# Moving an RMS gain from the weights to the transposed activations, and re-ordering the first batch, in a fused attention and SwiGLU kernel

## The chip, the cores and the metric

The kernel runs on one core of a Trainium2 chip. A core has five engines that run their own instruction streams in order and meet at semaphores: PE (TensorE, matmuls and transposes), DVE (VectorE), ACT (ScalarE), POOL (GpSimd) and SP (SyncE, which here only issues transfers). Transfers run on 16 DMA engines that all queues share. The metric is device time in microseconds (us) of one execution; lower is better.

## The reference

Selective attention over 8 batches, 8 heads, 576 positions and head size 64, followed by a SwiGLU feed-forward network (FFN) over the resulting 4608 tokens of width 512, with RMS normalisation and a gain `rms_g` in front of it:

```python
scores = scale * np.matmul(q, k.transpose(0, 1, 3, 2))
cum = np.cumsum(np.maximum(s, 0.0), axis=-1)
bias = -(cum[:, :, :, None] - cum[:, :, None, :])
scores = np.where(causal, -1000000000.0, scores + np.minimum(bias, 0.0))
...
attn = attn / (np.sum(attn, axis=-1, keepdims=True) + 1e-09)
x = np.matmul(attn, v)          # then tokens x (heads * 64)
rms = np.sqrt(np.mean(x * x, axis=-1, keepdims=True) + 1e-06)
xn = x / rms * rms_g
g = xn @ w_gate                 # 512 x 1536
silu = g * (1.0 / (1.0 + np.exp(-g)))
out = (silu * (xn @ w_val)) @ w_out
```

## The kernel before

**Units of work.** A batch is cut into five blocks of 128 positions (the last has 64). For each batch `b`:

- k and q arrive as fp32 over SP's queue (`load_kq`, `load_kq_tail`) in one buffer `kq32` for all batches, and are cast to bf16 in ten pieces (`cast`, L133, into `kqn`, which holds two batches). V arrives as bf16 over POOL's queue, one transfer a block (`load_v`, L137).
- Eight steps T (`t_step`, L146) transpose a pair of heads of k (w = 0) or q (w = 1) through PSUM into `kqT`: four PE transposes and one copy, on ACT or DVE (L154, L152). A tail step (L161, L164, L165) does the last 64 positions.
- S steps (`s_step`, L196) compute scores of a key block for four heads; ACT takes exp with the decay as a per-partition bias (L212) into `E`; POOL zeroes the causal corner with an affine select (L218), called the mask below.
- AV steps (`av_step`, L233, L239) multiply by V, with a column of ones for the sum. DVE divides (L246, L248), sums squares (L253), POOL raises mean square plus epsilon to the power -1/2 (L256, L259).
- `x_scale` (L266, DVE) applies that factor; an XT step (`xt_step`, L274) transposes the block through PSUM tile `psT`, and one DVE copy (L279) writes `xnT`, a ring that holds four FFN chunks.

The FFN runs in nine chunks of 512 tokens. A chunk has twelve pieces of 128 columns of the gate (L472, then tanh on ACT, L475) and of the value (L481), which DVE joins into `Ht` (L484, L477), and then four output tiles (L496) that ACT copies out (L501). Silu is written with tanh: g(1 + tanh(g/2))/2. The factor 1/2 and `rms_g` are multiplied into the weights by `scale_w` (L515, L518), one half of the columns at a time.

**Order.** Nothing is scheduled by a tool: the order on each engine is the order of the calls. The first part of the program (L585 to L693) is a list written by hand: transfers, setup of the decay (`decay_setup`, which ends in `biasK`), the first four blocks of batch 0, batch 1's casts and transposes. From there on attention is cut into steps that `step` places in the FFN's matmuls, one call of `step` being a slot; a chunk calls it 36 times. `can_t`, `can_s`, `can_av` and `can_xt` say which step may be placed, by lags counted in slots and not by any time. Before a chunk, `need` calls `step` until the XT step of the chunk's last token has been placed, which makes slots without FFN work. V transfers, casts and checks of the input's range (`check_mag`, `check_max`, results in `acc`) wait in side queues (`v_side`, `pool_side`, `dve_side`), from which a slot takes at most one each.

**PSUM.** `psF` has four buffers (FFN tiles, and pairs for early S steps); `psS`, `psAV` and `psT` have one buffer each. A step that writes into one of these waits on PE until its last reader has ended, and PE runs in order.

**A second path.** `general` computes the same without the range assumptions, and runs only if the checks fail; with these inputs it doesn't run.

Of the kernel before, what the change touches and what calls it, by code (L numbers as in the profile page):

```python
# [26 lines left out]
def kernel(  # L27
# [12 lines left out]
    nc = tc.nc  # L40
# [66 lines left out]

    def psT():
        return pp.tile([128, 8, 128], BF16, name="psT", tag="T", bufs=1)

    def psT32():
        return pp.tile([128, 512], FP32, name="psT32", tag="T", bufs=1)

# [21 lines left out]
    def load_v(b, c):  # L135
        n = rows(c)
        nc.gpsimd.dma_start(  # L137
            out=v_sb[0:n, b % 2, c, :, 0:64],
            in_=v[b, :, c * 128:c * 128 + n, :].rearrange("h p d -> p h d"))
# [130 lines left out]
    def xt_step(b, qb):  # L270
# [8 lines left out]
        nc.vector.tensor_copy(out=xnT[:, :, t0:t0 + m], in_=pX[:, 0:CC, 0:m])  # L279
        if m < n:  # L280
            nc.vector.tensor_copy(out=xnT[:, :, 0:n - m], in_=pX[:, 0:CC, m:n])
# [13 lines left out]
    SLOTS = 36  # L295
    slot = [0]
    done = {}
# [23 lines left out]
    def check(b):  # L321
        later(dve_side, 2, [f for w in (0, 1) for f in (
            lambda w=w: check_mag(b, w), lambda: check_max(0), lambda: check_max(1))]
            + [lambda: done.__setitem__(("check", b), slot[0])])
# [19 lines left out]
    def after_av(b):  # L344
        if b + 2 < B:
            later(v_side, 1, [lambda c=c: load_v(b + 2, c) for c in range(NSC)]
                  + [lambda: done.__setitem__(("V", b + 2), slot[0])])

    def do_t(key, **kw):
        b, hp, w = key  # L350
        if hp == "tail":
            tail_step(b)
            done["T", b] = slot[0]
            after_tail(b)
        else:
            t_step(b, hp, w, **kw)
# [26 lines left out]
    def can_t():  # L383
        if not t_seq or slot[0] - last["T"] < 2:
            return False
        b, hp, w = t_seq[0]
        return ready(2, "cast", b) and (b < 2 or ready(1, "S", b - 2, 4, 0))
# [14 lines left out]
    def can_av():  # L402
# [3 lines left out]
        if b > 1 and not ready(8, "V", b):  # L406
# [17 lines left out]
    def step():  # L424
# [9 lines left out]
        if v_side and slot[0] % 2:  # L434
# [29 lines left out]
    def ffn(c, extra=None):  # L464
        x0 = (c * DM) % RING
# [27 lines left out]
        for tb in range(4):  # L493
# [7 lines left out]
            nc.scalar.activation(out=osb, in_=Op, func=AF.Copy)  # L501
# [8 lines left out]

    def scale_w(i):

        fs = slice(i * (DF // 2), (i + 1) * (DF // 2))
        for cc in range(CC):
            nc.vector.tensor_scalar(out=wg_sb[:, cc, fs], in0=wg_sb[:, cc, fs],  # L515
                                    scalar1=rms_g_sb[:, cc:cc + 1], scalar2=None, op0=ALU.mult)
        for cc in range(CC):
            nc.vector.tensor_scalar(out=wv_sb[:, cc, fs], in0=wv_sb[:, cc, fs],  # L518
                                    scalar1=rms_g_sb[:, cc:cc + 1], scalar2=0.5,
                                    op0=ALU.mult, op1=ALU.mult)  # L520

    def decay_setup():
# [10 lines left out]
        ps = psT32()  # L533
# [49 lines left out]
    with tc.manual_schedule():  # L583

        load_kq(nc.sync, 0, 0, 0, 4)  # L585
        nc.scalar.dma_start(out=s_sb, in_=s.rearrange("b h s -> (b h) s"))
        load_kq(nc.scalar, 0, 1, 0, 4)
        load_kq(nc.sync, 0, 0, 4, 8)
        load_kq(nc.scalar, 0, 1, 4, 8)
        for w in (0, 1):  # L590
            load_kq_tail(nc.sync, 0, w)
        nc.sync.dma_start(out=rms_g_sb, in_=moe_rms_g.rearrange("(cc p) -> p cc", p=128))
        make_identity(nc, ident_f)
        make_identity(nc, ident_bf)
        nc.vector.memset(shf[:, 4, 64:128], 0.0)
        nc.vector.memset(v_sb[:, 0, :, :, 64:65], 1.0)
        nc.vector.memset(mhalf, -0.5)
        nc.vector.memset(stat, 0.0)
        nc.vector.memset(kq32[64:128, :, :, 256:320], 0.0)
        nc.vector.memset(ss_all, 0.0)  # L600
        nc.gpsimd.memset(E[:, 6:8, :, 192:256], 0.0)
        load_v(0, 0)
        decay_setup()
        for g in (0, 1):
            h0, h1 = 4 * g, 4 * g + 4
            for w in (0, 1):
                cast(nc.scalar, 0, w, 0, 1, h0, h1)
                cast(nc.vector, 0, w, 1, 2, h0, h1)
                cast(nc.gpsimd, 0, w, 2, 3, h0, h1)
                cast(nc.gpsimd, 0, w, 3, 4, h0, h1)  # L610
            load_v(0, 1 + g)
        load_w(moe_w_gate, wg_sb, 0)
        load_w(moe_w_val, wv_sb, 0)
        for w in (0, 1):
            cast(nc.gpsimd, 0, w, 4, 5)
        done["cast", 0] = 0
        load_v(0, 3)
        load_w(moe_w_gate, wg_sb, 1)
        load_w(moe_w_val, wv_sb, 1)
        for w in (0, 1):  # L620
            load_kq(nc.sync, 1, w)
            load_kq_tail(nc.sync, 1, w)
        nc.vector.memset(v_sb[:, 1, :, :, 64:65], 1.0)
        nc.vector.memset(v_sb[64:128, :, 4, :, 0:64], 0.0)
# [4 lines left out]
        t_seq[:] = [x for x in t_seq if x[0] > 1 or x[1:] == ("tail", 0)]  # L629
        t_seq.pop(0)  # L630
        scaled[0] = 4

        def t_first(b, g):
            for hp in (2 * g, 2 * g + 1):
                for w in (0, 1):
                    do_t((b, hp, w), pT=psF16() if w else psT())
# [4 lines left out]
        def s_first(kb, g, pair=None):  # L641
            do_s((0, kb, g), pair)()

        t_first(0, 0)
        s_first(0, 0)
        t_first(0, 1)
        s_first(0, 1, pairF())
        s_first(1, 0, pairF())
        do_av((0, 0, 0))
        do_av((0, 0, 1))  # L650
        s_first(1, 1)
        s_first(2, 0, pairF())
        do_av((0, 1, 0))
        x_scale(0, 0)
# [235 lines left out]
```

## Time and profile before

| | |
|---|---|
| median of three runs | 421.56 us (420.84 to 422.25) |
| the profiled execution | 420.97 us, of which 419.4 us are the span of the trace |
| PE busy | 371.8 us (89%) |
| DVE busy | 322.2 us (77%) |
| ACT busy | 217.8 us (52%) |
| POOL busy | 180.1 us (43%) |
| first FFN matmul | 47.17 us |
| first matmul of chunk 1 | 100.57 us |
| last PE work ends | 412.9 us |

The times of engines are sums of their instructions. A busy share over the whole span hides that the stages differ: the first 47 us hold no FFN work, the first chunk takes 53 us, and later chunks about 39. Over the span in 40 slices the page shows (one digit a slice, busy tenths; DMA is the mean share of the 16 transfer engines):

```profile
PE   1563779698999889999999999999999999999993
DVE  4458499899899699988897899979767966764740
...
DMA  9999985348931755629242630190020011001002
```

In lists in order of time, a line has the start, the length, the engine, the program's line, the operation, output<-input, the shapes and the count; in brackets stands how long the engine was idle before, and what ended that.

### The profile page before, as it was taken

How to read it: one execution, taken by the hardware profiler on the slowest of the kernel's cores; microseconds unless marked ns; L12 is line 12 of the kernel's file. 1: busy time of each engine (PE TensorE's matmuls, PEld its weight loads, DVE VectorE, ACT ScalarE, POOL GpSimd, SP SyncE). 2: the span in 40 equal slices, each digit the busy share in tenths (PEclk: the TensorE clock that was granted, in tenths of full speed). 3: DMA queues.
4: the chain of work that ended last, by engine and by line, in shares of the span. 5: the costliest groups of instructions: out<-in, count | busy, mean ns of one | idle time of the engine just before them, and what ended most of it. 6: DMA issues, size and time to landing. Idle time of an engine off the chain costs nothing. (4 is left out here: it accounts for less than half of the span.)

```text
span 419.4 us, 7416 instructions
## 1 busy us (share of the span) xinstructions
PE 371.8 (89%) x2679; PEld 183.2 (44%) x2679; DVE 322.2 (77%) x678; ACT 217.8 (52%) x516; POOL 180.1 (43%) x288
## 2 busy tenths in 40 slices
PE   1563779698999889999999999999999999999993
PEld 1342433344544444445445444444454445444441
DVE  4458499899899699988897899979767966764740
ACT  2661265652577647644765486558645753323321
POOL 6767727576717757535734575343221320000000
PEclk9999999899999999999999999999999999999998
DMA  9999985348931755629242630190020011001002
GB/s 241 215 232 256 178 135 36 22 135 211 150 115 50 233 70 50 208 79 81 76 153 76 64 21 25 65 69 2 27 76 2 2 50 52 1 29 73 1 28 80
DMA packets 72125, 38.46 MB, mean 92 GB/s; under 512 B 47440, under 2 KB 67408, under 8 KB 72080
## 3 DMA queue, kind: packets, MB, share of 16 engines
q0 software_dynamic: 41168, 9.44, 24.4%
q1 hardware_dynamic: 29776, 27.27, 20.9%
q10 hardware_dynamic: 1136, 1.20, 0.8%
q8 instruction: 23, 0.38, 0.4%
q14 instruction: 22, 0.18, 0.1%
HBM read 37.90 MB, written 9.44 MB: 113 GB/s over the span
## 5 line engine op out<-in xcount | busy, mean ns | idle before, releaser
L212 ACT ACTIVATE E<-psS,biasK 128x256 bf16<-128x256 f32 (+2 forms) x300 | 105.6, 434 | 33.3 <-PE psS L196 30.6
L472 PE MATMUL psF<-xnT,wg_sb 128*128 128x512 bf16 x432 | 111.9, 382 | 2.0 <-DVE xnT L279 1.1
L481 PE MATMUL psF<-xnT,wv_sb 128*128 128x512 bf16 x432 | 112.8, 384 | 0.5 <-DVE Ht L477 0.2
L496 PE MATMUL psF<-wout_sb,Ht 128*128 128x512 bf16 x432 | 104.9, 379 | 0.0
L475 ACT ACTIVATE T<-psF 128x512 f32<-128x512 f32 x108 | 64.7, 599 | 74.3 <-PE psF L472 62.8
L218 POOL TENSOR_SCALAR_AFFINE_SELECT E<-E 128x512 bf16<-128x512 bf16 x72 | 49.5, 688 | 99.9 <-ACT E L212 98.9
L484 DVE SCALAR_TENSOR_TENSOR U<-T,psF 128x512 bf16<-128x512 f32 x108 | 73.7, 683 | 18.3 <-ACT T L475 17.9
L477 DVE TENSOR_TENSOR Ht<-U,psF 128x512 bf16<-128x512 bf16 x99 | 67.5, 682 | 5.5 <-PE psT L146 0.5
L481 PEld LDWEIGHTS <-wv_sb 128*128 128x128 bf16 x432 | 39.3, 98 | 45.4 <-issue 6.9
L472 PEld LDWEIGHTS <-wg_sb 128*128 128x128 bf16 x432 | 38.1, 98 | 39.0 <-issue 7.2
L496 PEld LDWEIGHTS <-Ht 128*128 128x128 bf16 x432 | 37.8, 98 | 38.0 <-issue 2.7
L133 POOL CAST kqn<-kq 128x512 bf16<-128x512 f32 (+1 forms) x80 | 51.7, 669 | 4.0 <-DMA kq<-in_k_dram 2.3
L501 ACT ACTIVATE osb<-psF 128x512 f32<-128x512 f32 x36 | 21.6, 601 | 48.6 <-PE psF L496 45.0
L256 POOL TENSOR_SCALAR al_all<-ss_all 128x1 f32<-128x1 f32 (+1 forms) x40 | 15.9, 397 | 62.8 <-DVE xs_sb L253 62.2
L248 DVE TENSOR_TENSOR x_sb<-psAV,rZ 128x256 bf16<-128x256 f32 (+1 forms) x80 | 33.8, 423 | 2.7
L239 PE MATMUL psAV<-v_sb,E 128*128 128x65 bf16 x320 | 30.2, 199 | 5.9 <-POOL E L218 5.9
L137 POOL DMA_DIRECT2D v_sb<-in_v_dram x40 | 35.3, 889 | 0.0
L233 PE MATMUL psAV<-v_sb,E 128*128 128x65 bf16 x256 | 25.7, 198 | 6.9 <-DVE x_sb L248 6.9
L196 PE MATMUL psS<-kqT 64*128 64x256 bf16 (+2 forms) x300 | 25.7, 257 | 6.3 <-ACT E L212 4.9
L253 DVE SCALAR_TENSOR_TENSOR xs_sb<-x_sb 128x512 bf16<-128x512 bf16 (+1 forms) x40 | 29.7, 743 | 1.4
L154 ACT ACTIVATE kqT<-psT 128x512 bf16<-128x512 bf16 x32 | 19.4, 607 | 19.9 <-PE psT L146 19.9
L239 PEld LDWEIGHTS <-E 128*128 128x128 bf16 x320 | 22.8, 101 | 14.3 <-POOL E L218 6.4
(82 smaller groups left out, 318.2 us busy)
## 6 DMA issues: line engine op xcount, KB each, us to landing
out_dram<-osb SPq DMA_DIRECT2D x36, 256.0 KB, 2.0
kq<-in_k_dram SPq DMA_DIRECT2D x7, 1024.0 KB, 5.9
kq<-in_q_dram SPq DMA_DIRECT2D x7, 1024.0 KB, 6.7
v_sb<-in_v_dram POOLq DMA_DIRECT2D x32, 128.0 KB, 4.4
wg_sb<-in_moe_w_gate_dram POOLq DMA_DIRECT2D x2, 768.0 KB, 15.0
wv_sb<-in_moe_w_val_dram POOLq DMA_DIRECT2D x2, 768.0 KB, 19.5
wout_sb<-in_moe_w_out_dram POOLq DMA_DIRECT2D x1, 1536.0 KB, 14.7
kq<-in_k_dram SPq DMA_DIRECT2D x2, 512.0 KB, 5.2
```

Source lines behind the costliest of these rows:

```text
L133: eng.tensor_copy(out=o, in_=i)
L137: nc.gpsimd.dma_start(out=v_sb[0:n, b % 2, c, :, 0:64], in_=v[b, :, c * 128:c * 128 + n, :].rearrange("h p d -> p h d"))
L212: nc.scalar.activation(out=Ev[:, h - h0, 0:N], in_=pair[par][:, o:o + N], func=AF.Exp, scale=0.125, bias=biasK[:, kb, bh:bh + 1])
L218: nc.gpsimd.affine_select(out=Ev[:, :, 0:nq], in_=Ev[:, :, 0:nq], pattern=[[0, nh], [1, nq]], compare_op=ALU.is_ge, fill=0.0, base=0, chan ...
L239: nc.tensor.matmul(o, lhsT=d, rhs=v_sb[:, p, qb, h, :], start=(j == 0 and qb == 0), stop=(j == 3))
L248: nc.vector.tensor_tensor(out=xo[:, g * 256:(g + 1) * 256].rearrange("p (h d) -> p h d", h=4), in0=pv[0:n, :, 0:64], in1=rZ[0:n].unsqueeze ...
L472: nc.tensor.matmul(Gp, lhsT=wg_sb[:, cc, fs], rhs=xnT[:, cc, x0:x0 + DM], start=(cc == 0), stop=(cc == CC - 1))
L475: nc.scalar.activation(out=T, in_=Gp, func=AF.Tanh, scale=0.5)
L477: nc.vector.tensor_tensor(out=Ht[:, fb - 1, :], in0=pend[0], in1=pend[1], op=ALU.mult)
L481: nc.tensor.matmul(Vp, lhsT=wv_sb[:, cc, fs], rhs=xnT[:, cc, x0:x0 + DM], start=(cc == 0), stop=(cc == CC - 1))
L484: nc.vector.scalar_tensor_tensor(out=U, in0=T, scalar=1.0, in1=Gp, op0=ALU.add, op1=ALU.mult)
L496: nc.tensor.matmul(Op, lhsT=Ht[:, fb, tb * 128:(tb + 1) * 128], rhs=wout_sb[:, fb, :], start=(fb == 0), stop=(fb == FB - 1))
```

## The change

`scale_w` is gone. `rms_g` is applied where `xnT` is written: each of the four groups of 128 model columns has the gain as a per-partition scalar there, so a block's copy becomes four, two on ACT and two on DVE. The factor 1/2 rides in the copy of the output tile. The hand-written first part is re-ordered: casts of batch 0 split differently over the engines, transposes of heads 0 to 3 first, V transfers and weight transfers placed between other work on POOL, batch 1's k cast on ACT and q on POOL, batch 1's transposes left to the slots (with a lag of one slot, alternating between `psT` and the bank of `psAV`), some memsets on other engines, all first k and q loads on SP's queue. V's readiness is now kept for each block, the V queue may run in each of the first eight slots, and the checks' marker shares its last entry.

```diff
@@ xt_step
-        nc.vector.tensor_copy(out=xnT[:, :, t0:t0 + m], in_=pX[:, 0:CC, 0:m])
-        if m < n:
-            nc.vector.tensor_copy(out=xnT[:, :, 0:n - m], in_=pX[:, 0:CC, m:n])
+        for d0, j0, j1 in ((t0, 0, m), (0, m, n)):
+            if j1 == j0:
+                continue
+            for cc in range(CC):
+                o, i = xnT[:, cc, d0:d0 + j1 - j0], pX[:, cc, j0:j1]
+                if cc < 2:
+                    nc.scalar.activation(out=o, in_=i, func=AF.Copy, scale=rms_g_sb[:, cc:cc + 1])
+                else:
+                    nc.vector.tensor_scalar(out=o, in0=i, scalar1=rms_g_sb[:, cc:cc + 1],
+                                            scalar2=None, op0=ALU.mult)
@@ load_v
+        done["V", b, c] = slot[0]
@@ do_t
+            if b == 1 and (hp + w) % 2:
+                kw["pT"] = psAV16()
@@ can_t
-        if not t_seq or slot[0] - last["T"] < 2:
+        if not t_seq:
             return False
         b, hp, w = t_seq[0]
+        if slot[0] - last["T"] < (1 if b == 1 else 2):
+            return False
@@ can_av
-        if b > 1 and not ready(8, "V", b):
+        if not ready(8, "V", b, qb):
@@ step
-        if v_side and slot[0] % 2:
+        if v_side and (slot[0] % 2 or slot[0] < 9):
@@ ffn
-            nc.scalar.activation(out=osb, in_=Op, func=AF.Copy)
+            nc.scalar.activation(out=osb, in_=Op, func=AF.Copy, scale=0.5)
@@ the first part, after the change (transfers, memsets and setup cut)
+        for g in (0, 1):
+            for w in (0, 1):
+                load_kq(nc.sync, 0, w, 4 * g, 4 * g + 4)
...
+        piece(0, 0, (ACT, ACT, POOL, POOL))
+        decay_setup()
+        piece(1, 0, (ACT, DVE, POOL, POOL))
         load_v(0, 0)
+        do_t((0, 0, 0), pT=psT(), dve=True)
+        do_t((0, 1, 0), pT=psF16(), dve=False)
+        do_t((0, 0, 1), pT=psAV16(), dve=True)
+        do_t((0, 1, 1), pT=psF16(), dve=False)
+        piece(0, 1, (ACT, DVE, DVE, POOL))
         load_w(moe_w_gate, wg_sb, 0)
+        piece(1, 1, (ACT, DVE, DVE, POOL))
         load_w(moe_w_val, wv_sb, 0)
+        s_first(0, 0)()
...
+        load_v(0, 1)
+        s_first(0, 1, pairF())()
+        s_first(1, 1)()
         for w in (0, 1):
+            cast(POOL, 0, w, 4, 5)
+        do_av((0, 0, 0))
+        do_av((0, 0, 1))
+        load_v(0, 2)
+        s_first(2, 0, pairF())()
+        tail_step(0)
...
+        x_scale(0, 1)
+        load_w(moe_w_gate, wg_sb, 1)
+        do_av((0, 2, 0))
+        do_av((0, 2, 1))
+        load_w(moe_w_val, wv_sb, 1)
+        s_first(3, 1, pairF())()
+        do_xt((0, 1))
...
+        for r in range(NSC):
+            cast(ACT, 1, 0, r, r + 1)
+        x_scale(0, 2)
+        do_av((0, 3, 0))
+        do_av((0, 3, 1))
+        do_xt((0, 2))
+        nc.gpsimd.memset(v_sb[64:128, :, 4, :, 0:64], 0.0)
+        x_scale(0, 3)
+        for r in range(NSC):
+            cast(POOL, 1, 1, r, r + 1)
+        do_xt((0, 3))
...
+        later(v_side, 0, [
+            lambda: load_v(0, 4), lambda: load_v(1, 0), lambda: load_v(1, 1),
+            lambda: nc.gpsimd.dma_start(out=wout_sb,
+                                        in_=moe_w_out.rearrange("(fc p) d -> p fc d", p=128)),
+            lambda: load_v(1, 2), lambda: load_v(1, 3), lambda: load_v(1, 4)])
...
-            if fb == 3:
-                scale_w(1)
```

`piece(w, g, engines)` casts rows 0 to 3 of k (w = 0) or q (w = 1) for heads 4g to 4g + 3, one row on each engine named. The setup's PE transposes go to a `psF` buffer instead of `psT`. `general` gets the same treatment of `rms_g` and 1/2.

## The prediction

> **What bounds the kernel now.** I read the stretches first (busy time of each engine between marks that I set at the first feed-forward matmul, at the long stops of TensorE and at the start of chunk 1), then the order in time around each stop. Columns of the stretches: start:end, length, busy time (instructions) of PE, its weight loads, DVE, ACT, POOL, then granted clock, DMA share and GB/s.
>
> ```profile
> 0.00:47.17 47.17, 20.95 (x182) 14.56 (x183) 27.46 (x66) 19.29 (x46) 34.67 (x60) 1.00 1.15 235
> 47.17:59.67 12.50, 12.49 (x74) 5.19 (x72) 9.06 (x16) 7.55 (x22) 3.83 (x5) 1.00 1.43 155
> 59.67:62.07 2.40, 0.25 (x8) 0.26 (x9) 2.37 (x8) 0.79 (x3) 1.18 (x1) 1.00 0.40 66
> ...
> 75.80:78.67 2.87, 0.00 (x1) 0.00 (x1) 2.06 (x7) 2.84 (x10) 0.00 (x0) 0.91 0.68 43
> 78.67:100.57 21.90, 19.42 (x160) 9.58 (x160) 20.41 (x45) 9.94 (x27) 14.14 (x22) 0.93 0.52 155
> ```
>
> Two stages differ from the rest. Before 47.17 no FFN matmul runs and PE is busy 20.95 of 47.17 us. Chunk 0 (47.17 to 100.57, 53.4 us) is 14 us longer than a later chunk (about 39), with DVE busy 46.4 of it, so DVE is the nearest limit there. After 100.57 PE is busy all but some 6 us up to 413, so what is won or lost before 100.57 reaches the end almost whole.
>
> In the first stage POOL, DVE and PE show what stands in front of the FFN:
>
> ```profile
> 28.02 2.84 POOL L133 CAST kqn<-kq 128x512 bf16<-128x512 f32 x5
> 31.54 3.69 POOL L133 CAST kqn<-kq 128x512 bf16<-128x512 f32 x5 [0.69 <-DMA kq<-in_q_dram]
> 35.19 0.75 POOL L218 TENSOR_SCALAR_AFFINE_SELECT E<-E 128x512 bf16<-128x512 bf16 x1
> ```
> ```profile
> 32.97 2.48 DVE L515 TENSOR_SCALAR wg_sb<-wg_sb,rms_g_sb 128x768 bf16<-128x768 bf16 x4
> 35.37 1.76 DVE L518 TENSOR_SCALAR wv_sb<-wv_sb,rms_g_sb 128x768 bf16<-128x768 bf16 x4
> ```
> ```profile
> 35.99 0.24 PE L239 MATMUL psAV<-v_sb,E 128*128 128x65 bf16 x1 [3.79 <-POOL E L218]
> ...
> 43.96 0.61 PE L274 MATMUL psT<-ident_bf,xs_sb 128*128 128x128 bf16 x4 [1.51 <-DVE xs_sb L266]
> 45.09 0.59 PE L146 MATMUL psT<-ident_bf,kqn 128*128 128x128 bf16 x4 [0.52 <-DVE xnT L279]
> ```
>
> The reader sees batch 1's ten casts ahead of a mask on POOL, so that attention-times-V waits 3.79 us; DVE scaling weights (4.24 us) just after; and batch 1's transposes (L146) ahead of the FFN.
>
> **The change, part by part.**
>
> *Start of the FFN.* The last exps of batch 0's first four blocks end at 33.0 (31.64 + 1.36). With no casts, weight scaling or batch-1 transposes in between, the chain from there is: mask 0.65, AV 0.4, L246 + L248 + L253 at 0.18 + 0.42 + 0.83, power (L256, L259) 0.82, L266 0.6, transposes 0.6, then the new copies to xnT about 1.0 (below): 5.5 us, so 38.5. The first stage also starts sooner. All casts and transposes of heads 0 to 3 are placed first: biasK is ready at 9.67 as now (the s transfer is the same), one cast on DVE 0.42, two pairs of transposes 1.1, copy 0.6, so the first score matmul comes at 11.8 instead of 13.37, 1.6 us sooner. That gives 37.0. ACT's five new casts (128x512; the POOL rows give 0.6 to 0.74, I take 0.6: 3.0 us) lie after the last exps and end about when the third block's transposes are ready: nothing, and up to 2 us if ACT is late. POOL keeps five casts, now behind the last power and a memset of V (L624's row: 0.9): 4.6 us. They begin 2.2 us before the FFN (L266, transposes, copies) and the second slot needs them 3.4 us after its start (rows at 47.17 and 48.87, 1.7 each): 5.6 us of cover; what exceeds it stops PE one for one. Memsets that change engines: acc (POOL 2.23) goes to DVE's 2.98 idle before s lands, about 1.1 by L599's row; kqT's goes to DVE, about 0.5, in front of an L266 that waits for the power: nothing.
>
> *Queues.* The first four k and q loads all go to SP's queue, s alone to ACT's. They landed at 5.7 to 10.9 and move the same bytes, without V piece 0 beside them; the casts they feed wait for biasK at 9.67. I take nothing, bounds -1 and +0.5. wout is now issued on POOL behind the mask of slot 3, near 47, and lands 14.7 later (its row); the output matmuls are 36 us behind the start, at 74: hidden.
>
> *The V transfers.* POOL's queue shows one order. I asked for each transfer by its issue time; the last column is us to landing, issue times 13.39 and 15.24:
>
> ```profile
> wv_sb<-in_moe_w_val_dram POOLq DMA_DIRECT2D x1, 768.0 KB, 13.5
> ...
> v_sb<-in_v_dram POOLq DMA_DIRECT2D x1, 128.0 KB, 16.6
> ```
>
> So a V piece issued behind two weight halves landed at 31.8, 4.9 us after the half before it (26.9); the half before that landed at 22.0, 4.1 after the V piece before. Now V piece 1 moves from ahead of the weights to behind them (issue about 16.5). Weights are issued near 9 and 10, piece 0 lands about 12, the halves about 16 and 21, piece 1 between 22.2 (five V pieces issued from 44.5 land 1.2 apart) and 25.9 (the 4.9). PE wants it at 22.5: late by 0 to 3.4 us, and everything in that row of work with it. I take 1.5, as batch 1's q is stuck behind the k tail until POOL's tail casts and is only starting then. FFN start: 37.0 + 1.5 = 38.5, a gain of 8.7 (bounds 5.5 to 11). The second weight halves, issued near 30 and 31, land by 45 with the same 5 us each; the FFN reads them 15 us after its start: hidden.
>
> *Chunk 0.* Out: the second weight scaling, 2.8 us of DVE (58.5 to 61.2), PE's stop of 2.4. In: eight transpose steps of batch 1, PE 0.22 each when warm (102.30 to 102.52) = 1.8, four copies on DVE of 0.69 = 2.8, four on ACT. DVE is unchanged and DVE limits: I take 0; bounds -2.4 (only PE counts as stopped) and +1.8 (only PE's work counts). The steps alternate between psT and psAV; twice one follows a user of the same buffer by one slot or less, so PE can stand for a DVE copy (0.7 each), inside these bounds.
>
> *xnT.* Forty copies of 128x512 (0.41) or 128x256 (0.28) become two on ACT and two on DVE. The two DVE sizes give 0.15 + 0.0005 per element, 0.2 for 128 columns: two cost 0.4, nothing new. ACT's exps at 64 and 192 columns take 0.22 and 0.34 each in a row, so 0.28 for 128, 0.56 a block, on an engine busy 52%. The wait is what matters. The tail step already has this form, ACT and DVE reading one psT:
>
> ```profile
> 28.00 0.38 ACT L164 ACTIVATE kqT<-psT 128x256 bf16<-128x256 bf16 x1 [0.71 <-PE psT L161]
> ```
> ```profile
> 28.41 0.29 DVE L165 COPY kqT<-psT 128x256 bf16<-128x256 bf16 x1 [1.52 <-ACT kqT L164]
> ```
>
> DVE starts only when ACT has ended, though both only read. So a block's copies take 0.56 + 0.4 = 1.0 in place of 0.41, and DVE, with Ht and U queued behind, stands for up to 0.6 a block; PE waits for U and Ht through psF. Where DVE lags, it finds ACT done and pays nothing. In chunk 0 (four blocks, two of DVE's largest users around) I take 0.3 each, 1.2; in the other chunks DVE has 23.7 us idle from 100.57 to 294, so most is covered: 1.0. Bounds 0 and 5.
> [...]
>
> *Boundary to chunk 1.* The planner's rules, followed slot by slot, put batch 1's attention later: the FFN's chunk 1 begins at slot 40 instead of 37 (a chunk fills 36), chunk 2 at 77 instead of 76. Empty slots leave PE to the chain AV, L246 to L266, transposes, xnT. Now that stop is 0.96 + 0.68 us (99.5 to 100.57). I take +1.0 (bounds 0 and 2.5), and -0.5 where the next boundary loses two empty slots. A stop can also cool PE: after 2.92 us idle, four matmuls took 1.89 instead of 1.03 and the whole stretch 1.3 more, after 2.4 idle they took 1.02. [...]
>
> *Nothing:* the 0.5 at the output rides in an ACT copy that is there anyway (L501, 0.60).
>
> Sum: -8.7 + 0 + 1.2 + 1.0 + 1.0 - 0.5 = -6.0. The profiled execution took 420.97 (span 419.4 and 1.6 around it), so 415.0; the median of the runs is 0.6 above that execution: **415.6**.
>
> **The rivals.**
> 1. *V late* (15%). Piece 1, then pieces 2 and 3, land as late as the 4.9 rows allow, and the FFN starts at 42: gain 2.5, 419. For: two halves ahead in one queue. Against: they are issued 3 us sooner than now.
> 2. *DVE was not the limit of chunk 0* (20%). The removed stop counts (-2.4), copies hide, start at 37: 415.6 - 1.5 - 2.4 - 1.2 = 410.5. For: PE stopped exactly while L515 and L518 ran. Against: DVE 93% busy from 78.67 on.
> 3. *The ACT-to-DVE order on psT makes it slower* (7%). 36 blocks in the FFN stage; if each leaves DVE standing 0.35 that PE feels, 12.6 in place of 2.2, giving 426. It decides from about 0.25 a block, where the 8.2 us won otherwise are eaten. For: DVE is 85 to 93% busy to 294. Against: ACT is idle 38% there and usually first.
> 4. *Moved work only* (3%): stops reappear in chunk 0, about 421.
>
> **How the numbers follow.** My forecast has 55%, by itself 412.5 to 418.5. The range 410 to 420.5 takes in most of rivals 1 and 2 and leaves out rival 3 and a start near 36. A difference under 0.3% (1.3 us) can't be told from none. Faster: 55 + 20 + 11 of rival 1; same: 4 of rival 1 and 3 of rival 4; slower: rival 3.
>
> **What would show it.** The first FFN matmul near 38.5; the AV of block 1 in batch 0 naming a V transfer as releaser for 0 to 3 us; DVE's xnT pieces naming ACT; no stop of 2.4 us in chunk 0; chunk 1 starting 93 to 95. Wrong if the FFN starts after 42, or if chunk 0 exceeds 57 us.

## The result

| | before | after |
|---|---|---|
| median | 421.46 us | 429.0 us (428.18 to 429.2) |
| ratio to before, 95% interval | | 1.0174 [1.0152, 1.0196] |
| profiled execution / its span | 420.97 / 419.4 us | 428.18 / 426.6 us |
| first FFN matmul | 47.17 us | 43.92 us |
| chunk 0 | 53.40 us | 56.83 us |
| chunks 1 to 8 | 312.30 us | 318.11 us |
| end of PE's work to end of the span | 6.5 us | 7.7 us |

The change makes the kernel 1.7% slower, where 1.4% faster was predicted. The rows of the table account for the 7.2 us between the two spans: -3.25 + 3.43 + 5.81 + 1.2. The FFN does start sooner, but chunk 0 takes the same time back, and the later chunks lose nearly 6 us more.

The stretches of the kernel after, cut at the first FFN matmul of a chunk (start:end, length, busy time and instructions of PE, its weight loads, DVE, ACT, POOL, granted clock, DMA share, GB/s):

```profile
0.00:43.92 43.92, 16.95 (x150) 10.85 (x151) 22.77 (x59) 20.98 (x54) 24.25 (x47) 1.00 1.00 194
43.92:100.75 56.83, 45.28 (x352) 21.91 (x352) 47.31 (x104) 32.76 (x88) 30.95 (x47) 1.00 0.89 153
100.75:146.18 45.43, 42.99 (x312) 20.73 (x312) 38.04 (x76) 29.19 (x75) 25.96 (x41) 0.96 0.60 127
146.18:194.12 47.94, 42.49 (x340) 20.88 (x340) 40.72 (x98) 28.39 (x74) 22.64 (x40) 1.00 0.45 93
194.12:418.86 224.74, 223.09 (x1531) 106.56 (x1528) 170.43 (x372) 127.21 (x315) 64.07 (x110) 1.00 0.24 48
```

And chunks 1 and 2 (rows 3 and 4) in the kernel before:

```profile
100.57:144.47 43.90, 41.33 (x317) 20.68 (x316) 36.64 (x69) 28.22 (x67) 26.49 (x41) 1.00 0.57 119
144.47:189.41 44.94, 42.26 (x341) 20.96 (x341) 42.30 (x92) 25.22 (x62) 25.10 (x38) 1.00 0.52 113
```

Of the 5.8 us that chunks 1 to 8 lose, 1.5 fall in chunk 1, 3.0 in chunk 2 and 1.3 behind it. PE has the same work in chunk 2 (42.3 and 42.5 us), and DVE has even less (40.72 instead of 42.30), yet the chunk is 3.0 us longer. DVE's list of waits for that stretch of the kernel after names what is new (us in total, times, longest):

```profile
DVE xnT L295 <- ACT xnT L293: 5.5, 5, 1.5
```

40.72 busy and 5.5 standing make 46.2 of 47.94. Before, DVE had 2.6 us to spare in this chunk. Over the whole of the kernel after, the page's groups of the new copies read (line, engine, operation, count, busy us, mean ns, idle before and what ended it):

```profile
L293 ACT ACTIVATE xnT<-psT,rms_g_sb 128x128 bf16<-128x128 bf16 (+1 forms) x84 | 25.4, 364 | 10.4 <-PE psT L282 9.5 <-DVE xnT L295 1.0
...
L295 DVE TENSOR_SCALAR xnT<-psT,rms_g_sb 128x128 bf16<-128x128 bf16 (+1 forms) x84 | 19.1, 268 | 25.7 <-ACT xnT L293 23.3 <-PE psAV L247 2.4
```

DVE stands 23.3 us for ACT in all: 2.8 of it in chunk 0, 1.6 in chunk 1, 5.5 in chunk 2 and 11.2 behind that, where slack covers most of it. A piece takes DVE 0.268 us and ACT 0.364 by the mean of one; two in a row overlap, so 84 of them make only 19.1 and 25.4 us busy, 0.23 and 0.30 a piece.

Chunk 1 loses its 1.5 us in another way. There DVE is busy only 38.0 of 45.4 us, but PE's granted clock is 0.96 on average where it was 1.00: it was 0.50 from 100.98 to 104.39, after the stops of 1.52, 0.69 and 0.46 us at the boundary to this chunk. Four matmuls at 102.58 took 1.91 us, and 1.03 from 104.57 on.

The first stage shows the other loss. PE's stops in the kernel after, in order of time (start, length; in brackets the idle time before it and what ended that):

```profile
27.83 0.21 PE L247 MATMUL psAV<-v_sb,E 128*128 128x65 bf16 x1 [5.51 <-DMA v_sb<-in_v_dram]
...
38.68 0.24 PE L241 MATMUL psAV<-v_sb,E 128*128 128x65 bf16 x1 [2.41 <-DVE x_sb L256]
...
42.86 0.61 PE L282 MATMUL psT<-ident_bf,xs_sb 128*128 128x128 bf16 x4 [3.12 <-DVE xs_sb L274]
...
43.92 1.44 PE L491 MATMUL psF<-xnT,wg_sb 128*128 128x512 bf16 x3 [0.46 <-ACT xnT L293]
```

PE stood 5.51 us for V piece 1. The DMA issues between 9.5 and 11.5 us in that kernel, and then the one of V piece 1 at 16.22 us (size, us to landing), tell why:

```profile
wg_sb<-in_moe_w_gate_dram POOLq DMA_DIRECT2D x1, 768.0 KB, 8.9
wv_sb<-in_moe_w_val_dram POOLq DMA_DIRECT2D x1, 768.0 KB, 13.4
v_sb<-in_v_dram POOLq DMA_DIRECT2D x1, 128.0 KB, 3.8
...
v_sb<-in_v_dram POOLq DMA_DIRECT2D x1, 128.0 KB, 11.6
```

The halves of the weights, issued at 9.99 and 11.08, landed at 18.9 and 24.5, and V piece 1 after both, at 27.8. V piece 0, ahead of them, took 3.8 us.

### The profile page after: what moved, and what is told of

Read it like the earlier page. It is cut to its first block, busy times and chain, and to the rows that moved or that the text cites. A ratio compares the mean times of both kernels' runs of the same rounds, so it can differ in the third digit from the quotient of the medians.

```text
span 426.6 us, 7571 instructions
## 1 busy us (share of the span) xinstructions
PE 370.8 (87%) x2679; PEld 180.9 (42%) x2679; DVE 319.3 (75%) x706; ACT 239.1 (56%) x604; POOL 167.9 (39%) x282
## 5 line engine op out<-in xcount | busy, mean ns | idle before, releaser
L226 POOL TENSOR_SCALAR_AFFINE_SELECT E<-E 128x512 bf16<-128x512 bf16 x72 | 47.2, 655 | 93.8 <-ACT E L220 93.2
L140 POOL CAST kqn<-kq 128x512 bf16<-128x512 f32 (+1 forms) x73 | 48.1, 680 | 3.2 <-DMA kq<-in_k_dram 3.1
L264 POOL TENSOR_SCALAR al_all<-ss_all 128x1 f32<-128x1 f32 (+1 forms) x40 | 11.6, 290 | 87.5 <-DVE xs_sb L261 84.6
L295 DVE TENSOR_SCALAR xnT<-psT,rms_g_sb 128x128 bf16<-128x128 bf16 (+1 forms) x84 | 19.1, 268 | 25.7 <-ACT xnT L293 23.3
L241 PEld LDWEIGHTS <-E 128*128 128x128 bf16 x256 | 20.3, 100 | 28.4 <-DVE x_sb L256 17.2
L293 ACT ACTIVATE xnT<-psT,rms_g_sb 128x128 bf16<-128x128 bf16 (+1 forms) x84 | 25.4, 364 | 10.4 <-PE psT L282 9.5
## 6 DMA issues: line engine op xcount, KB each, us to landing
wv_sb<-in_moe_w_val_dram POOLq DMA_DIRECT2D x2, 768.0 KB, 11.6
```

Source lines behind the costliest of these rows:

```text
L140: eng.tensor_copy(out=o, in_=i)
L226: nc.gpsimd.affine_select(out=Ev[:, :, 0:nq], in_=Ev[:, :, 0:nq], pattern=[[0, nh], [1, nq]], compare_op=ALU.is_ge, fill=0.0, base=0, chan ...
L241: nc.tensor.matmul(o, lhsT=E[:, eslot[b, qb - 1, g], j, 128:256], rhs=v_sb[:, p, qb - 1, h, :], start=(j == 0), stop=False)
```

## The experiments

Lengths below are from the one profiled execution of each kernel (start of the FFN; chunk 0; chunks 1 to 8), and stretches in which PE's clock fell to 0.50 lie at other places in each (one from 78.1 to 81.6 us in the kernel before, one from 101.0 to 104.4 in the kernel after), so a difference of less than a microsecond between two profiles says little; times and ratios with their 95% interval are against the kernel before on the same chip. Each diff is against the kernel after unless another is named.

**Which half of the change costs what.** The first two runs split the change: the gain in the old order, and the new order with the old scaling of the weights.

`gain_only`, against the kernel before: `xt_step`'s four pieces, 0.5 at the output, no `scale_w`.

```diff
-        nc.vector.tensor_copy(out=xnT[:, :, t0:t0 + m], in_=pX[:, 0:CC, 0:m])
...
+            for cc in range(CC):
...
+                if cc < 2:
+                    nc.scalar.activation(out=o, in_=i, func=AF.Copy, scale=rms_g_sb[:, cc:cc + 1])
+                else:
+                    nc.vector.tensor_scalar(out=o, in0=i, scalar1=rms_g_sb[:, cc:cc + 1],
+                                            scalar2=None, op0=ALU.mult)
...
-        scale_w(0)
...
-            if fb == 3:
-                scale_w(1)
```

> The kernel before with the gain moved to the copies into xnT (two on ACT, two on DVE) and no scaling of the weights; the old order everywhere else. Theory A (the shared psT bank makes DVE stand behind ACT at each block, and that is what chunks 0 to 2 lost): the 2.4 us stop in chunk 0 goes and the first stage gains 1 to 2, but 6 to 8 us are lost behind them, so 423 to 426. Theory B (the loss is in the new order: V behind the weights, batch 1's transposes and the later slots in chunk 0): this kernel only loses the weight scaling, 416 to 418.5.

Measured: 425.26 us, 1.0096 [1.0065, 1.0127]; start 47.05, chunk 0 52.19, chunks 1 to 8 317.8. The time lies in the range of theory A, although the first stage gained only 0.1 us. So most of the loss of the later chunks goes with the gain: +5.5 in the old order, and +5.0 in the new one (318.1 against the 313.1 of `order_only`, next). In chunk 0 the gain is worth -1.2: DVE's busy time falls by 2.8 there, while PE's clock was 0.50 for 6.8 us of the chunk where it was 3.4 before.

`order_only`: the kernel after with `scale_w` and the old copy.

```diff
-            for cc in range(CC):
...
+        nc.vector.tensor_copy(out=xnT[:, :, t0:t0 + m], in_=pX[:, 0:CC, 0:m])
...
+        scale_w(0)
...
+            if fb == 3:
+                scale_w(1)
```

> The changed kernel's order with the weights scaled as before (scale_w(0) after the second XT step, scale_w(1) in chunk 0) and one DVE copy into xnT without the gain. Theory A: chunks 1 to 3 take 44, 45 and 40 us as before; the first stage still stands for V 5 us, scale_w is back, about 420 to 423. Theory B: the loss stays, 428 or more.

Measured: 429.15 us, 1.0174 [1.0123, 1.0225]; start 46.26, chunk 0 61.05, chunks 1 to 8 313.1. That is theory B: the new order by itself wins only 0.9 us at the start and loses 7.65 in chunk 0. PE's longest stop there, in the order of time of this kernel:

```profile
63.73 0.61 PE L154 MATMUL psAV<-ident_bf,kqn 128*128 128x128 bf16 x4 [4.33 <-DVE x_sb L256]
```

A transposing step of batch 1 that borrows `psAV` waits for the divide of an AV step, and that divide lies behind the weight scaling (58.71 to 61.8) and an input check on DVE. The clock fell here too: it was 0.50 for 11.6 us of this chunk, against none on record in the kernel after, and PE's busy time is 49.6 us instead of 45.3. Chunk 1, without any of the new copies, is as long as in the kernel after (45.66 and 45.43), again at a lower clock (0.94). Moved from the first stage into chunk 0, these steps meet DVE's queue. The two halves of the change don't add: by the end of PE's work the gain is +4.2 in the old order and -1.5 in the new one, as the removed scaling relieves the very stretch that the new order loads.

**The xnT copies.** Four kernels keep the gain and change who makes the copies.

`dve1`: one DVE instruction with the gain as a broadcast operand.

```diff
-            for cc in range(CC):
...
+            nc.vector.tensor_tensor(
+                out=xnT[:, :, d0:d0 + j1 - j0], in0=pX[:, 0:CC, j0:j1],
+                in1=rms_g_sb.unsqueeze(2).to_broadcast([128, CC, j1 - j0]), op=ALU.mult)
```

> The changed kernel with the four copies of a block made one DVE multiplication by the gain as a broadcast operand, no ACT. DVE 0.6 to 0.7 us a block in place of 0.47, but no wait for ACT. Theory A: chunks 0 to 2 win back 6 to 8 us, 421 to 424. Theory B: no change, 428 to 430.

Measured: 425.67 us, 1.0116 [1.0065, 1.0167]; start 44.19, chunk 0 57.96, chunks 1 to 8 314.3. DVE is busy longer with the copies (25.3 us, where its two pieces took 19.1) and no longer waits for ACT; the later chunks lose 2.0 against before instead of 5.8. As chunk 0 grew by 1.1, the time lies between the two that were expected.

`act4`: all four pieces on ACT.

```diff
-                if cc < 2:
+                if cc < 4:
```

> The changed kernel with all four pieces of a block's copy on ACT, none on DVE. If the loss after chunk 0 is DVE standing behind ACT on the shared bank, DVE loses both the wait and 19 us of work: chunk 2 falls from 47.9 to 45 or less, 422 to 425 in all. If the loss is ACT's added work (tanh and exp later), ACT has 25 us more of it: chunks 1 and 2 no shorter, 429 to 433.

Measured: 419.26 us, 0.9974 [0.9958, 0.999]; start 43.26, chunk 0 54.66, chunks 1 to 8 311.65. The edit of one character takes the ratio from 1.0174 to 0.9974, level with the kernel before within 0.4% and nearly 3 us below what was expected for this case. Chunk 2 in this kernel:

```profile
142.56:186.45 43.89, 41.90 (x340) 20.94 (x340) 37.93 (x82) 30.98 (x88) 23.81 (x40) 1.00 0.49 102
```

DVE has 37.93 busy and no copy that stands for ACT's; ACT has 2.6 us more to do than in the kernel after and is still far from full.

`stt`: the gain goes into the scaling by the RMS factor (`x_scale`, one instruction with two multiplications), and `xnT` gets its old single copy.

```diff
-        nc.vector.tensor_scalar(
+        nc.vector.scalar_tensor_tensor(
...
-            scalar1=al_all[0:n, col:col + 1], scalar2=None, op0=ALU.mult)
+            scalar=al_all[0:n, col:col + 1], in1=g_row[0:n, :], op0=ALU.mult, op1=ALU.mult)
...
-            for cc in range(CC):
...
+        nc.vector.tensor_copy(out=xnT[:, :, t0:t0 + m], in_=pX[:, 0:CC, 0:m])
```

> The changed kernel with the gain multiplied in ahead of the transposes: x_scale multiplies by the token's factor and by a row of gains that one transfer spreads over the partitions; one DVE copy into xnT as before the change, no ACT. DVE pays 0.69 for 0.34 to 0.69 a block. If the form of the copies is the cause of the 5.8 us lost after chunk 0, chunks 1 to 8 take 312 to 313.5 in place of 318.1 and the whole 422.5 to 424.5; if DVE's work and not the wait decides, 426 to 428.

Measured: 431.63 us, 1.0252 [1.0205, 1.0298]; start 44.21, chunk 0 58.56. A miss, and a useful one: no copy is shared here, yet it is the slowest of these. The groups of this instruction in `stt` and then in the kernel before:

```profile
L275 DVE SCALAR_TENSOR_TENSOR xs_sb<-x_sb,al_all,g_row 128x512 bf16<-128x512 bf16 (+1 forms) x40 | 36.7, 916 | 10.1 <-POOL al_all L268 10.1
```
```profile
L266 DVE TENSOR_SCALAR xs_sb<-x_sb,al_all 128x512 bf16<-128x512 bf16 (+1 forms) x40 | 21.2, 529 | 8.1 <-POOL al_all L259 8.0
```

It costs DVE 15.5 us more. This fits DVE's whole time, busy or standing, as what counts, with the form of the copies as one way to lengthen it.

`dve_first`: the runs above took work from DVE as well as its wait. This one turns the order of the pieces round and leaves all work as it is.

```diff
-            for cc in range(CC):
+            for cc in (2, 3, 0, 1):
```

> The changed kernel with the order of the four xnT pieces turned round: DVE's two are issued ahead of ACT's two, so that ACT stands behind DVE on the PSUM tile and DVE behind nobody; the work of each engine is the same. If DVE's standing behind ACT is what lengthens chunks 1 to 8, they come to about 312.5 to 314.5 us together (318.1 in the changed kernel) and the time to 423.5 to 426.5 us. If the price lies in DVE's and ACT's own longer copies, or in the two copies being one after the other for the matmuls that read them, chunks 1 to 8 stay within 1 us of 318.1 and the time at 428 to 430 us.

Measured: 426.9 us, 1.0151 [1.011, 1.0192]; start 43.90, chunk 0 58.44, chunks 1 to 8 314.7. The waits of this kernel:

```profile
ACT xnT L293 <- DVE xnT L295: 24.1, 21, 2.5
...
DVE xnT L295 <- ACT xnT L293: 1.3, 2, 0.6
```

The wait has changed sides: 24.1 us of ACT's time where it was 23.3 of DVE's. With DVE's work unchanged (18.9 us in its pieces) the later chunks get 3.4 us shorter, so that much of their 5.8 is DVE's standing itself. Nearly all of it comes back in chunk 2 (45.75 instead of 47.94) and behind it (1.0); chunk 1 stays long (45.26), with PE's clock at 0.50 for its first 3 us. So of the 2.4 us that are left against before, 1.4 lie in chunk 1 and 1.0 behind it, for which the longer copies on both engines are the likeliest cause; that is not shown. The total falls short of what was expected by 0.4 us, because chunk 0 grew by 1.6: at the boundary to chunk 1 ACT, and PE behind it, now wait until DVE has passed an input check and made its pieces (a stop of 2.13 us before the first matmul of chunk 1, where it was 0.46).

**The V transfers.** `v_first` issues V pieces 1 and 2 ahead of the first halves of the weights.

```diff
+        load_v(0, 1)
         piece(0, 1, (ACT, DVE, DVE, POOL))
+        load_v(0, 2)
         load_w(moe_w_gate, wg_sb, 0)
...
-        load_v(0, 1)
...
-        load_v(0, 2)
```

> The changed kernel with V pieces 1 and 2 issued ahead of the first weight halves, as before the change. The stop of 5.5 us on the V transfer at 22.3 goes. Both theories: the first FFN matmul comes 4 to 5.5 us sooner, near 39. If the FFN stage does not depend on when it starts, 424 to 425; if the second weight halves, batch 1's casts or the loads of batch 2 are then late, less is won, down to nothing (429).

Measured: 424.86 us, 1.0091 [1.0067, 1.0115]; start 38.94, chunk 0 57.21, chunks 1 to 8 318.35. The start moves 5.0 us forward, and 4.4 of it reach the end of PE's work. What stands in the way now is V piece 3, still behind the weights:

```profile
32.41 0.21 PE L247 MATMUL psAV<-v_sb,E 128*128 128x65 bf16 x1 [2.35 <-DMA v_sb<-in_v_dram]
```

**Batch 1's transposes.** `kt_first` makes the four k transposes of batch 1 ahead of the FFN again, copied by ACT; the list of steps left to the slots loses them, and of the four that stay two use the bank of `psAV`.

```diff
-            if b == 1 and (hp + w) % 2:
+            if b == 1 and w == 1 and hp % 2 == 0:
...
+        for hp in range(HP):
+            do_t((1, hp, 0), pT=psF16(), dve=False)
         do_xt((0, 3))
```

> The changed kernel with the four k steps of batch 1's transposes put back ahead of the FFN, into the 3.1 us in which PE waits for the last block's scaling; copies on ACT. If the transposes in the slots lengthen chunk 0 (56.8 against 53.4), half of that goes: chunk 0 near 54.5, start at most 0.6 later, 426 to 427.5. If the later slots of batch 1's attention do it by themselves, 428.5 to 429.5, as they move by only two slots.

Measured: 430.94 us, 1.0266 [1.0232, 1.03]; start 43.03, chunk 0 55.69, chunk 1 49.24 (45.43 after). Chunk 0 is 1.1 us shorter, but chunk 1 loses 3.8. In the order of time at its start:

```profile
100.18 2.98 DVE L274 TENSOR_SCALAR xs_sb<-x_sb,al_all 64x512 bf16<-64x512 bf16 x1 [0.71 <-POOL al_all L267]
100.66 0.95 POOL L145 DMA_DIRECT2D v_sb<-in_v_dram  x1
101.62 0.62 POOL L140 CAST kqn<-kq 128x512 bf16<-128x512 f32 x1
102.17 0.88 POOL L145 DMA_DIRECT2D v_sb<-in_v_dram  x1
...
103.40 1.01 PE L491 MATMUL psF<-xnT,wg_sb 128*128 128x512 bf16 x2 [4.04 <-DVE xnT L295]
```

One DVE instruction of 64x512 took 2.98 us, where the one at the same place in the kernel after (102.24) takes 0.96 and the one in its chunk 2 takes 0.34. The long stop was followed by a low clock too: 0.50 for 6.8 us of chunk 1, against 3.4 in the kernel after. This was not foreseen; the time is 1.4 us above the slower of the two expectations, and it spoils the run as a test of the transposes.

`combo` puts `stt`, all V pieces ahead of the weights and `kt_first` together.

> The three together: gain in x_scale, all four V pieces of batch 0 ahead of the weight halves, batch 1's k transposes ahead of the FFN. If the three causes are separate, the FFN starts near 37.5 to 39, chunk 0 takes 53 to 55, the rest 312 to 313.5: 411 to 416. If chunk 0 stays near 57, 416 to 418.

Measured: 429.41 us, 1.0204 [1.0175, 1.0233]; start 39.27, chunk 0 62.14. This is far from both expectations. The start gains what the V pieces promise, and DVE's longer work takes it back in chunk 0. The same long instruction stands at its boundary to chunk 1 (3.01 us at 98.01, and a stop of 5.14 on PE).

`gain_act4`, against the kernel before: the gain with all pieces on ACT, in the old order.

```diff
-        nc.vector.tensor_copy(out=xnT[:, :, t0:t0 + m], in_=pX[:, 0:CC, 0:m])
...
+            for cc in range(CC):
...
+                if cc < 4:
+                    nc.scalar.activation(out=o, in_=i, func=AF.Copy, scale=rms_g_sb[:, cc:cc + 1])
...
-        scale_w(0)
```

> The old order of the work (batch 0 and 1 transposed as before, old V places) with gain in the PSUM copies and half at the output, weights not scaled, all four xnT pieces on ACT. DVE loses the whole scaling of the weights and its half of the xnT copies, and keeps nothing that stands behind ACT. Theory A (DVE's busy and standing time sets chunks 0 to 3, and the new order is what lengthens chunk 0): start at about 47 us, chunk 0 at 49 to 51 us instead of 53.4 before, chunks 1 to 8 about 311 to 312 together, 414 to 416.5 us in all. Theory B (the order is neutral in chunk 0): chunk 0 at about 54.5 as in the version with the new order, 418.5 to 420 us.

Measured: 416.5 us, 0.9889 [0.9859, 0.9919]; start 46.78, chunk 0 48.50, chunks 1 to 8 311.8. The gain at the copies is good for 1.1% by itself, if DVE has no part in it. Beside `act4` it prices the new order: 3.5 us won at the start, 6.2 lost in chunk 0. Chunk 0 of `gain_act4`, then of `act4`:

```profile
46.78:95.28 48.50, 42.66 (x310) 20.05 (x315) 42.44 (x90) 31.32 (x90) 26.91 (x39) 0.96 0.80 120
```
```profile
43.26:97.92 54.66, 45.09 (x352) 22.09 (x352) 45.81 (x92) 35.00 (x98) 31.02 (x47) 0.98 0.92 164
```

PE has 2.4 us more to do there, DVE 3.4, ACT 3.7, POOL 4.1: what was moved out of the first stage arrives in a stretch where PE and DVE were 88% busy already.

`tact_only` and `act4_v_tact` give the copies of batch 1's transposes to ACT; `act4_v` is `act4` with the V pieces as in `v_first`.

```diff
+            if b == 1:
+                kw["dve"] = False
```

> The changed kernel with the four copies of batch 1's q and k transposes that DVE makes (0.69 us each) given to ACT, and nothing else. If DVE's time in chunk 0 sets its length, chunk 0 falls by 2.5 to 3.5 us from 56.8 and the time to 425.5 to 427 us. If ACT, which has two xnT pieces per block here, is then late itself, DVE's standing grows by as much and the time stays at 428 to 429.5 us.

> The changed kernel with all four xnT pieces on ACT and V pieces 1 and 2 issued ahead of the first halves of the weights. If the two gains are of different stretches they add: start at about 38.5 us (5 us less than with the V pieces behind the weights), chunk 0 still 54.7, chunks 1 to 8 about 311.7, 414 to 415.5 us. If the earlier start only brings chunk 0 to the work that DVE still owes, chunk 0 grows by 2 to 4 us and the time is 416.5 to 418.5 us.

> The version before this one, with the copies of batch 1's q and k transposes out of PSUM all on ACT (half of them were on DVE, 0.69 us each, four). If those copies behind DVE's other work are what lengthens chunk 0, chunk 0 falls from 54.7 to about 52 us and the time is 412 to 413.5 us; if the transposes' bank waits or PE's own work set it, it stays within 0.5 us of the version before this one, or is up to 1.5 us slower because ACT is then late for the exponentials.

Measured:

| | us | ratio | start | chunk 0 | chunks 1 to 8 |
|---|---|---|---|---|---|
| `tact_only` | 427.46 | 1.0132 [1.0107, 1.0157] | 44.72 | 55.54 | 318.5 |
| `act4_v` | 417.08 | 0.9896 [0.9848, 0.9944] | 39.94 | 56.35 | 311.7 |
| `act4_v_tact` | 414.1 | 0.9817 [0.979, 0.9844] | 39.95 | 53.40 | 312.1 |

The transposes' copies on DVE are worth 1.3 us of chunk 0 in the kernel after (56.83 to 55.54). The start was 0.8 later in that execution, which ends PE's work where it did without the edit (418.8); by its time `tact_only` lies between its two expectations and decides neither. `act4_v_tact` is 0.6 us above the first of its own, with 2.95 us less in chunk 0 than `act4_v`. But only a part of that is the copies, as the next lines show: against `act4`, which has the same chunk but for them, it is 1.3 again.

`act4_v` misses its first expectation by 1.6 us. Its time is that of the second, but for other reasons than DVE's debt. The start came at 39.94 instead of 38.5, as PE still stood 3.1 us for V piece 3; and chunk 0 grew by 1.7 against `act4`, although DVE's busy time there is the same (45.9 and 45.8): the matmuls themselves took longer, at two places. The first is the beginning of the chunk. Its first ten microseconds in `act4_v`, then in `act4`:

```profile
39.94:49.94 10.00, 8.81 (x52) 4.46 (x53) 6.12 (x9) 5.01 (x16) 6.43 (x9) 0.78 1.38 268
```
```profile
43.26:53.26 10.00, 9.03 (x60) 4.55 (x60) 6.92 (x11) 5.62 (x17) 7.38 (x10) 0.88 1.23 283
```

The clock of 0.50 lasted for the first 4.4 us of the chunk in the one and 2.4 in the other. The second tanh of the chunk starts 0.95 us later, counted from the chunk's first matmul, and all that follow, to the eleventh, are late by as much. The second place comes after that. In the order of time of `act4_v`, then of `act4`:

```profile
70.99 0.20 PE L241 MATMUL psAV<-v_sb,E 128*128 128x65 bf16 x1 [1.74 <-DVE x_sb L256]
...
72.32 1.86 PE L500 MATMUL psF<-xnT,wv_sb 128*128 128x512 bf16 x4 [0.92 <-DVE Ht L496]
...
74.66 1.89 PE L491 MATMUL psF<-xnT,wg_sb 128*128 128x512 bf16 x4
```
```profile
73.37 0.20 PE L241 MATMUL psAV<-v_sb,E 128*128 128x65 bf16 x1 [1.74 <-DVE x_sb L256]
...
74.70 1.02 PE L500 MATMUL psF<-xnT,wv_sb 128*128 128x512 bf16 x4 [0.91 <-DVE Ht L496]
```

The same two stops, 1.74 and 0.92, are followed in the one by groups of four matmuls of 1.86 and 1.89 us and in the other by one of 1.02. The granted clock was 0.50 from 72 to 78 us in `act4_v` and 1.00 in `act4`. The twelfth tanh is 2.8 us late, and at the end of the chunk 1.7 are left, 0.75 of them from this place.

`act4_vall` is `act4` with all four V pieces ahead of the weights, and `act4_vall_tact` has the transposes' copies on ACT too.

```diff
+        load_v(0, 1)
...
         piece(0, 1, (ACT, DVE, DVE, POOL))
+        piece(1, 1, (ACT, DVE, DVE, POOL))
+        load_v(0, 2)
+        load_v(0, 3)
         load_w(moe_w_gate, wg_sb, 0)
-        piece(1, 1, (ACT, DVE, DVE, POOL))
         load_w(moe_w_val, wv_sb, 0)
...
-        load_v(0, 1)
...
-        load_v(0, 2)
...
-        load_v(0, 3)
```

> The changed kernel with all four xnT pieces on ACT and all four V pieces of batch 0 issued ahead of the weights. If the V pieces' landing is all that the first stage waits for, the start is at 37 to 38.5 us and the time 413 to 415 us; if the weights' landing then comes too late, the first matmul of the FFN waits for a weight half, the start is at 39.5 to 42 us and the time 416 to 418 us.

> All three repairs together: four xnT pieces on ACT, all V pieces of batch 0 ahead of the weights, batch 1's transposes copied by ACT. If the three lie in different stretches they add: start 37.8 us, chunk 0 53 to 53.5 us, chunks 1 to 8 311.5 to 312.2 us, 409.5 to 411.5 us in all. If chunk 0 is bound by PE's own work and ACT by then, the earlier start or the lighter DVE is lost there and the time is 412.5 to 415 us.

Measured: `act4_vall` 415.12 us, 0.9849 [0.9824, 0.9873], start 37.83, chunk 0 54.74, chunks 1 to 8 311.7; `act4_vall_tact` 411.99 us, 0.9772 [0.9756, 0.9788], start 38.43, chunk 0 53.16, chunks 1 to 8 311.9. In both, no stop names a V transfer any more and the weights are there in time. The copies are worth 1.6 us of chunk 0 between these two. The second, the fastest of all, is 0.5 us above what was expected of its time; its three parts in the profile came as expected within 0.7 us. Against the kernel after they are -5.5 at the start, -3.7 in chunk 0 and -6.2 later: together 15.4 us at the end of PE's work.

## Why the prediction was wrong

It said 415.6 and the kernel takes 429.0: on the scale of the profiled execution 415.0 and 428.2, 13.2 us apart. Two terms of its sum failed: the wait for V piece 1, taken as 1.5 us, and DVE's wait on `psT` in the later chunks, taken as mostly covered. A third, the clock after the boundary's stops, stood beside the sum and not in it. Its steps account for the difference:

| step | predicted | measured | off by |
|---|---|---|---|
| start of the FFN | 38.5 | 43.92 | 5.4 |
| chunk 0 with the boundary to chunk 1 | +2.2 | +3.4 | 1.2 |
| chunks 1 to 8 | +0.5 | +5.8 | 5.3 |
| after PE's last work | 0 | +1.2 | 1.2 |

**The start: V piece 1 mis-sized.** The mechanism was in the text, with 1.5 us for it and a bound of 3.4; the stop measured 5.51, and `v_first` gave 5.0 us back. PE wanted the piece at 22.3, as predicted (22.5), and the piece came 3.3 us behind the second half, inside the row's 4.9. What was wrong is when the halves land: 18.9 and 24.5 where about 16 and 21 were taken, each issued a microsecond later. The prediction stacked them on the landing of piece 0 (12, measured 12.4) by the distances of the kernel before, 4.1 and 4.9 us; the distances came out as 6.5 and 5.6. Counted from their issue the halves were no slower than before: 8.9 and 13.4 us, against 9.3 and 13.5 there, the second of which stands in the prediction's own row. Had it counted so, from 10 with 13.5 and 4.9, piece 1 would have come up to 5.9 us late. The rest of the step's chain nearly holds: the first score matmul came at 11.74 (11.8 predicted), and the FFN, predicted at 37.0 without the V term, starts at 38.94 with two V pieces ahead of the weights and a stop of 2.35 for the third, and at 37.83 in `act4_vall`.

**The later chunks: "most is covered".** The step saw that DVE would wait for ACT on `psT`, had the size of a wait right (up to 0.6 a block; 23.3 us over 40 blocks is 0.58), and then let 23.7 us of idle time, summed from 100.57 to 294, cover it. Slack did not carry from one chunk to another: chunk 2 had 2.6 us and got 5.5 of standing, and lost 3.0; behind it only 1.3 were lost with 11.2 of standing. `gain_only` showed 5.5 lost in the old order, and `dve_first` that at least 3.4 of the 5.8 goes when only the wait changes sides. That a lagging DVE finds ACT done and pays nothing held for a part of the blocks only: there were 25 waits, with up to 2.1 us each. The sizes of the pieces were nearly right: in a row 0.23 for DVE's instead of 0.2, and 0.30 for ACT's instead of 0.28.

**Chunk 1: the halved clock.** 1.5 of the 5.8 us lie in chunk 1, and standing is not most of it: 0.5 is the longer stop at the next boundary, which falls at this chunk's end, and the rest is mostly clock. The stops at the first boundary, none over 1.52 us, were followed by a clock of 0.50 for 3.4 us. The prediction had this price (its row's 1.3, behind a stop of 2.92) beside the sum, where only the boundary's upper bound of 2.5 has room for it; here it came behind shorter stops. `act4` has the same order and a clock of 1.00 there; its second tanh of the chunk starts 3.14 us after the first matmul, against 4.88 in the kernel after, and 0.8 of the difference is left at the end of the chunk (44.64 and 45.43).

**Chunk 0: the sign of the parts.** "DVE is unchanged and DVE limits: I take 0" was near for the sum and wrong in its parts, which cancelled in part. `gain_only` and `gain_act4` show that the weight scaling and the old copies leaving DVE are worth 1.2 and 4.9 us; the new order costs 4.6 to 7.65 (`after` against `gain_only`, `order_only` against before, the latter with much of the chunk at half the clock), inside which 1.3 to 1.6 are DVE's copies of the transposes (`tact_only`, `act4_vall_tact`); no run separates the transposes from what else the order moves. The predicted boundary stop of +1.0 was right as a stop: 0.96 + 0.68 became 1.52 + 0.69 + 0.46. The next boundary was to save 0.5 and cost 0.5 (0.50 + 0.44 became 1.45).

**The rivals.** Two came true at once, each a part. Rival 1 had the right transfer, with a start at 42 where 43.92 was measured. Rival 3 had the right mechanism; its price of 12.6 was too high, its 0.25 us a block was not even reached (5.8 us over the 36 blocks after chunk 0's four is 0.16), and it decided nevertheless, because the 8.2 us that should have stood against it were eaten by rival 1's wait and chunk 0. Rival 2, that DVE was not the limit of chunk 0, is neither: each run that took work from DVE (`gain_only`, `act4`, `tact_only`, `gain_act4`) shortened chunk 0, but `act4_vall_tact` has there the DVE time of `gain_act4` (42.8 and 42.4 us) and is 4.7 us longer, 2.6 of them PE's longer busy time, so DVE is not the only limit in the new order. The fault in the chances was to treat the rivals as exclusive, so that the case with both had no weight.

**Left open.** The 1.2 us after PE's last work: the kernel before has 6.5 there and the sixteen others 6.9 to 7.9, `order_only`, without the factor at the output, among them with 7.5; nothing was tried on it. Also open is in what proportion the 1.0 us that `dve_first` leaves in chunks 2 to 8 belongs to ACT's or DVE's longer pieces, and why the clock fell after a stop in one kernel and not after the same stop in another.

## What to carry to other kernels

Hold a new wait against the slack of the very stretch in which it falls, engine by engine, and count standing as busy: here a chunk with 2.6 us of DVE's time to spare got 5.5 of standing and was 3.0 longer. Price a stop of PE with the clock that may follow it, as short stops here (1.52, 0.69 and 0.46 us) were followed by half the clock for 3.4 us. When two engines share the reading of one PSUM tile, in this program the second stands for the first (DVE 23.3 us for ACT in the kernel after, ACT 24.1 for DVE in `dve_first`); give the whole tile to the engine that has room, even if the copies take longer there (a piece 0.364 us on ACT and 0.268 on DVE; `act4` was faster even so). And in one DMA queue small pieces that are needed soon belong ahead of big ones that are needed later: here three transfers of 128 KB moved in front of the weights took 5.3 us off the end of PE's work (`act4` to `act4_vall`).

## What the runs showed of the hardware

- One DVE instruction took several times its usual length at one place. L274 on 64x512 took 2.98 us in `kt_first`, and its counterpart with two multiplications 3.01 in `combo`, each while POOL issued V transfers (0.95 and 0.88 us) and made casts without a gap. At the same place in `dve_first`, beside one V transfer of 0.95 us, L274 took 0.96; in the kernel after it took 0.96 there and 0.34 to 0.57 in the later batches, and the counterpart took 0.92 on average over its two shapes in `stt`. The delay lasted over several of POOL's instructions; no run separates the two engines, so its cause is not shown.
- The same two short stops of PE (1.74 and 0.92 us, with eight small matmuls of 0.2 us between them) were followed by a lower clock in one kernel and not in another: 0.50 for 7 us in `act4_v`, 1.00 in `act4`, which set the next pieces back by 1.9 us and the chunk by 0.75. In the kernel after, stops of 1.52, 0.69 and 0.46 were followed by 0.50 over 3.4 us. A stop of a given length had no fixed price here.
- A gain was not free in the DVE copy out of PSUM: the copy took 0.607 us on average as a `tensor_tensor` with a broadcast gain (`dve1`) and 0.384 as a plain copy before.
